# Gate, up and down products of a transformer block in one region with a fixed order of engines, shared accumulators and spread operand sums

## The chip, the cores and the metric

The kernel runs on one core of one Trainium2 chip. The metric is the device time of one execution in microseconds, the median of several. A profile is one execution; its span is a few microseconds off the median.

Engines are named as in the profile: PE is TensorE's matrix products, PEld its weight loads, DVE VectorE, ACT ScalarE, SP SyncE, which issues the transfers. A name such as L753 is a line of the kernel.

## The reference, cut to what matters

One transformer block over 2048 tokens of 1024 features, in bfloat16: a linear-attention part, then a gated feed-forward part of 3584 features. The change touches only the second part.

```python
def _B_ref(x, W_gate, W_up, W_down):
    gate = jnp.einsum("bsd,df->bsf", x, W_gate)     # (2048,1024) @ (1024,3584)
    up = jnp.einsum("bsd,df->bsf", x, W_up)
    gate = gate * (gate > 0)
    h = gate * up
    return jnp.einsum("bsf,fd->bsd", h, W_down)     # (2048,3584) @ (3584,1024)

h2 = h + _B_ref(_layernorm(h), W_gate, W_up, W_down)
```

## The kernel before

All large products use Strassen's scheme in Winograd's form: of two 2x2 block matrices, 7 block products and sums of operands and results instead of 8 products. So TensorE is not the only busy engine: VectorE makes sums of operands ahead of the products and adds accumulators to saved copies ("snaps") behind them.

**Gate/up.** There are 24 windows. One window is 7 products ("1" to "7") of 8 matmuls of 128x512 each. Product 1 goes to accumulator A, is copied out (a snap), and 6, 7 and 4 are added into the same A, with a snap after 6 and after 7. Product 2 goes to D; 5 and later 3 go to E. Each accumulator holds 128x1024 float32 values in PSUM; I call its place a pair of banks, one half for gate and one for up. A alternates between two places; D and E have one place each. `prev` is the last part of the previous window, put between the first and second part of this one. `fill` holds sums that the down product will want; one is taken per window from the fifth on. A scheduler decides each engine's order from this text. The results are stored to DRAM ("spilled") and loaded again by down as its operand x.

```python
    apools = [ps2, ps2b]                                   # A alternates, D and E do not
    def part1():
        st["A"] = A = apools[k % len(apools)].tile([P, 2, SW], FP32, tag="A", name="A")
        prod(A, 1, True)
        m1 = snap(A)                                       # ScalarE copy
        Dp = ps2.tile([P, 2, SW], FP32, tag="D", name="Dp")
        prod(Dp, 2, True)
        finish_sum(Dp, m1, 0)                              # VectorE: gu = D + m1, then hq = relu(gate)*up
    def part2():
        A = st["A"]
        prod(A, 6, False)
        st["u2"] = snap(A)
        st["E"] = E = ps2.tile([P, 2, SW], FP32, tag="E", name="E")
        prod(E, 5, True)
        prod(A, 7, False)
        finish_sum(E, snap(A), 3)
    def part3():
        ...  # product 4 into A and its result, product 3 into E, finish_sum(E, st["u2"], 1)
    # ... (cut) ...
        for s, f, wt_, fi in items:
            p1, p2, p3 = quad_steps(s, f, w[fi] if w else sums(wt_, fi), k)
            k += 1
            p1()
            if prev:
                prev()
            p2()
            if k > 4 and fill:
                fill.pop(0)()
            prev = p3
```

**Down.** Seven outer products, in the order 1, 2, 6, 5, 7, 3, 4. Two of them (1 and 7) are plain: 4 accumulators of 28 matmuls of 128x512, half of them before and half after the second half of the operands. The other five are Strassen again: 7 products of 28 matmuls of 128x256. Their operand sums (t1 to t4 of weights, s1 to s4 of activations) are made on VectorE from tiles loaded just before, in this order, and taken from a list `pend` at fixed places:

```python
        return [
            lambda: tt(out=t1, in0=b12, in1=b11, op=ALU.subtract),
            lambda: tt(out=t2, in0=b22, in1=t1, op=ALU.subtract),
            lambda: tt(out=s1, in0=a21, in1=a22, op=ALU.add),
            ...  # s2, s3, t3, t4, s4
        ]
    # ... (cut) ...
        if k in INNER:
            p1, p2, p3 = inner(op, *plans[k])
            p1()
            if prev:
                prev()
            some(3)
            p2()
            some(8)
            prev = p3
```

An output piece (a "sink" in the code) is two VectorE sums (`o` = accumulator + snap, then + the residual) and a store issued on the SP queue.

Of the kernel before, what the change touches and what calls it, by code (L numbers as in the profile page):

```python
# [31 lines left out]
def block_kernel(ctx: ExitStack, tc: tile.TileContext, x, wqkv, wo, wg, wu, wd, out, H: int):  # L32
# [542 lines left out]
    def weight_sums(w_sb, fi, nm):  # L575

        b = [[w_sb[:, k * KH:(k + 1) * KH, h, fi * P:(fi + 1) * P] for h in range(2)] for k in range(2)]
        t = tpool.tile([P, 4, KH, P], FP16, tag=nm, name=nm)
        nc.vector.tensor_tensor(out=t[:, 0], in0=b[0][1], in1=b[0][0], op=ALU.subtract)
        nc.vector.tensor_tensor(out=t[:, 1], in0=b[1][1], in1=t[:, 0], op=ALU.subtract)  # L580
        nc.vector.tensor_tensor(out=t[:, 2], in0=b[1][1], in1=b[0][1], op=ALU.subtract)
        nc.vector.tensor_tensor(out=t[:, 3], in0=b[1][0], in1=t[:, 1], op=ALU.subtract)
        return b[0][0], b[1][0], b[1][1], t[:, 3], t[:, 0], t[:, 1], t[:, 2]
# [3 lines left out]
    def wd_sums(c):  # L587

        raw = spool[0].tile([P, 2, 2, D], BF16, tag="wraw", bufs=1, name="wraw")
        for k in range(2):  # L590
            nc.sync.dma_start(out=raw[:, k], in_=wd_k[:, k, 2 * c:2 * c + 2, :])
        t = spool[0].tile([P, 4, 2, DW], FP16, tag="wt", bufs=1, name="wt")
        (b11, b12), (b21, b22) = [[raw[:, k, :, j * DW:(j + 1) * DW] for j in range(2)] for k in range(2)]
        nc.vector.tensor_tensor(out=t[:, 0], in0=b12, in1=b11, op=ALU.subtract)
        nc.vector.tensor_tensor(out=t[:, 1], in0=b22, in1=t[:, 0], op=ALU.subtract)
        nc.vector.tensor_tensor(out=t[:, 2], in0=b22, in1=b12, op=ALU.subtract)
        nc.vector.tensor_tensor(out=t[:, 3], in0=b21, in1=t[:, 1], op=ALU.subtract)
        for k in range(4):
            nc.sync.dma_start(out=t_dram[k][:, 2 * c:2 * c + 2, :], in_=t[:, k])
# [21 lines left out]
    def early_sums(f):  # L621

        k, r = divmod(f, FQ)
        hq = new_hq()
        nc.sync.dma_start(out=x1[0][k][:, r, :], in_=raw_dram[0][:, f, :])
        for q, j in ((3, H22), (2, H21), (1, H12)):
            nc.sync.dma_start(out=hq[:, j, :], in_=raw_dram[q][:, f, :])
        hh_sums_a(hq, 0, f)
        hh_sums_b(hq, 0, f)

    def quad_steps(s, fc, w, k):

        left = left_ops(hnT[s], hns[s])

        def prod(ps, m, start):
            for v in range(2):
                for kc in range(KH):
                    nc.tensor.matmul(ps[:, v, :], lhsT=w[v][m - 1][:, kc, :], rhs=left[m - 1][:, kc, :],  # L638
                                     start=(start and kc == 0), stop=(kc == KH - 1), skip_group_check=True)

        slots = {1: H12, 2: H21, 3: H22}
        is_early = k is None
        hq = None if is_early else new_hq()

        def dst(q):
            if is_early:
                return mwork.tile([P, SW], BF16, tag="hh1", bufs=4, name="hh1")[:]
            if q in slots:
                return hq[:, slots[q], :]
            return x1[s][fc // FQ][:, fc % FQ, :]  # L650

        def spill(q, ap):
            if is_early:
                nc.sync.dma_start(out=raw_dram[q][:, fc, :], in_=ap)
            elif q == 2:
                hh_sums_a(hq, s, fc)
            elif q == 1:
                hh_sums_b(hq, s, fc)

        def snap(ps):  # L660
            m = mwork.tile([P, 2, SW], FP32, tag="snap", bufs=4, name="snap")
            nc.scalar.copy(out=m[:], in_=ps[:])  # L662
            return m

        def finish_sum(ps, m, q):
            gu = mwork.tile([P, 2, SW], BF16, tag="gu", name="gu")
            nc.vector.tensor_tensor(out=gu[:], in0=ps[:], in1=m[:], op=ALU.add)  # L667
            d = dst(q)
            nc.scalar.activation(out=gu[:, 0, :], in_=gu[:, 0, :], func=ACT.Relu)  # L669
            nc.vector.tensor_tensor(out=d, in0=gu[:, 0, :], in1=gu[:, 1, :], op=ALU.mult)  # L670
            spill(q, d)

        st = {}

        def narrow():

            gus = {}

            def mm(ps, m, v, start):
                for kc in range(KH):  # L680
                    nc.tensor.matmul(ps[:], lhsT=w[v][m - 1][:, kc, :], rhs=left[m - 1][:, kc, :],
                                     start=(start and kc == 0), stop=(kc == KH - 1), skip_group_check=True)

            def fin(i, j, v, ps, m):
                q = 2 * i + j
                if v == 0:
                    gus[q] = mwork.tile([P, 2, SW], BF16, tag="gu", name="gu")
                gu = gus[q]
                if m is not None:
                    nc.vector.tensor_tensor(out=gu[:, v, :], in0=ps[:], in1=m, op=ALU.add)  # L690
                if v == 0:
                    nc.scalar.activation(out=gu[:, 0, :], in_=ps[:] if m is None else gu[:, 0, :], func=ACT.Relu)
                else:
                    d = dst(q)
                    nc.vector.tensor_tensor(out=d, in0=gu[:, 0, :], in1=ps[:] if m is None else gu[:, 1, :], op=ALU.mult)
                    spill(q, d)

            return strassen(pspool, mwork, mm, fin, 4)

        def part1():  # L700
            st["A"] = A = apools[k % len(apools)].tile([P, 2, SW], FP32, tag="A", name="A")
            prod(A, 1, True)
            m1 = snap(A)
            Dp = ps2.tile([P, 2, SW], FP32, tag="D", name="Dp")
            prod(Dp, 2, True)
            finish_sum(Dp, m1, 0)

        def part2():
            A = st["A"]
            prod(A, 6, False)  # L710
            st["u2"] = snap(A)
            st["E"] = E = ps2.tile([P, 2, SW], FP32, tag="E", name="E")
            prod(E, 5, True)
            prod(A, 7, False)
            finish_sum(E, snap(A), 3)

        def part3():
            A, E = st["A"], st["E"]
            prod(A, 4, False)
            rg = mwork.tile([P, SW], BF16, tag="rg", name="rg")  # L720
            nc.scalar.activation(out=rg[:], in_=A[:, 0, :], func=ACT.Relu)
            d = dst(2)
            nc.vector.tensor_tensor(out=d, in0=A[:, 1, :], in1=rg[:], op=ALU.mult)  # L723
            spill(2, d)
            prod(E, 3, False)
            finish_sum(E, st["u2"], 1)

        return narrow if k is None else (part1, part2, part3)

    def sums(wt, fi):  # L730
        return [weight_sums(wt[0], fi, "tg"), weight_sums(wt[1], fi, "tu")]
# [3 lines left out]
    for f in range(NE):  # L735
        st = {}

        def begin(f=f, st=st):
            st["q"] = quad_steps(0, f, sums(early[f // GP], f % GP), None)()
            next(st["q"])  # L740

        flow += [begin] + [lambda st=st: next(st["q"])] * 5
# [13 lines left out]
    ps2ctx = ExitStack()  # L756
    ps2 = ps2ctx.enter_context(tc.tile_pool(name="ps2", bufs=1, space=PSUM))
    apools = [ps2, ps2ctx.enter_context(tc.tile_pool(name="ps2b", bufs=1, space=PSUM))]
    x1pool = ctx.enter_context(tc.tile_pool(name="x1pool", bufs=4, side="right"))
    prepool = ctx.enter_context(tc.tile_pool(name="prepool", bufs=1, side="right"))  # L760
    sctx = ExitStack()
    spool.append(sctx.enter_context(tc.tile_pool(name="spool", bufs=1, side="right")))
# [4 lines left out]
    x1 += new_x(x1pool)  # L767

    todo = [[(1, f, early[f // GP], f % GP)] for f in range(NE)]
    todo += [[(s, g * GP + fi, g, fi) for s in range(NS) for fi in range(GP)] for g in range(NE // GP, FH // GP)]  # L770
    fill = [lambda f=f: early_sums(f) for f in range(NE)] + [lambda c=c: wd_sums(c) for c in range(FH // 2)]
    prev, k = None, 1
    for n, items in enumerate(todo):
        w = {}
        if n >= NE:
            wt, loads = load_group(items[0][2])
            for f in loads:
                f()
            w = {fi: sums(wt, fi) for fi in range(GP)}
# [3 lines left out]
        for s, f, wt_, fi in items:  # L783
            p1, p2, p3 = quad_steps(s, f, w[fi] if w else sums(wt_, fi), k)
            k += 1
            p1()
            if prev:
                prev()
            p2()
            if k > 4 and fill:  # L790
                fill.pop(0)()
            prev = p3
# [291 lines left out]
```

## Time and profile before

| | before |
|---|---|
| median time, three executions | 771.17 us (767.87 to 772.5) |
| span of the profiled run | 767.4 us |
| first matmul of gate/up starts at | 298.2 us |
| last matmul of gate/up | 601.7 us |
| last matmul | 761.4 us |
| holes of TensorE in gate/up | 13.3 us |
| holes of TensorE in down | 4.4 us |

The page gives TensorE's busy share:

```profile
PE 728.2 (95%) x4004; PEld 380.7 (50%) x4004; DVE 557.8 (73%) x1019; ACT 327.0 (43%) x597; POOL 6.1 (1%) x44
```

At 95% there seems to be little left. But the matmuls overlap in the record, so busy time is not work. I read starts instead: in the timeline a 128x512 matmul follows the last one after 0.216 us, a 128x256 one after 0.109 us, and what is above that is a hole. That is how all holes of this document are computed. (A group of matmuls in the timeline shows the idle time after the last one ended, which is 0.16 to 0.17 us less than the hole.)

The waits of TensorE, by what ended them; the columns are total us, number, longest us (only waits from 0.2 us or so are listed, so the sums are smaller than the holes):

```profile
engine line waited for: us in total, times, longest us
...
PE E L638 <- DVE gu L667: 5.0, 9, 1.5
...
PE accA L919 <- DVE snap L925: 2.8, 4, 1.3
...
PE A L638 <- DVE hq L723: 2.0, 5, 0.8
...
PE A L638 <- ACT snap L662: 1.1, 1, 1.1
```

L638 are the gate/up products: they wait for VectorE to free E (its sum `gu`) or A (`hq`). Two such holes in the timeline (start, length, engine, line, operation, count, and in brackets the idle time before with what ended it):

```profile
start us, us, engine line op out<-in xcount [idle before <-releaser]
...
380.37 1.02 PE L638 MATMUL A<-hn,wg 128*128 128x512 bf16 x4 [0.78 <-DVE hq L723]
...
383.85 1.02 PE L638 MATMUL E<-hs,tg 128*128 128x512 f16 x4 [1.16 <-DVE gu L667]
```

E's new product 5 waits for the sum that reads the old product 3 out of the same banks, because only one other product lies between them. And VectorE isn't always prompt. This is the view of stretches of 50 us (busy us of each engine with its number of instructions, the granted clock, the share of the transfer engines, GB/s):

```profile
core 0: us, PE busy (x) PEld busy (x) DVE busy (x) ACT busy (x) POOL busy (x), PEclk, DMA share, GB/s
...
350.00:400.00 50.00, 47.61 (x218) 21.13 (x217) 42.47 (x86) 20.42 (x27) 0.00 (x0) 1.00 0.94 307
...
450.00:500.00 50.00, 49.25 (x227) 21.95 (x226) 32.86 (x61) 21.25 (x29) 0.00 (x0) 1.00 0.35 106
...
600.00:650.00 50.00, 48.97 (x329) 32.02 (x328) 30.74 (x29) 5.59 (x7) 0.00 (x0) 1.00 0.86 320
```

VectorE is busy for 42.5 of 50 us at 350 to 400 us, where the down sums are bunched, and for 32.9 us at 450 to 500 us. TensorE runs 218 and 227 matmuls in these stretches, where 231 would fit.

### The profile page before, as it was taken

The page shows a single profiled execution, that of the slowest core. Times are in us where ns is not written, and L with a number is a line of the kernel's source. Part 1 is how long each engine was busy: PE and PEld are TensorE (multiplying, and loading weights), DVE is VectorE, ACT ScalarE, POOL GpSimd, SP SyncE. Part 2 cuts the span into 40 slices and gives each one's busy share as a digit, 9 for nine tenths or more (in the row PEclk, how much of TensorE's full clock was granted, in tenths as well). Part 3 has the DMA queues.
Part 4 walks back from the last instruction along what each step waited for, and adds up shares of the span by engine and source line. Part 5 has one row for each costly group of instructions (what it writes and reads, how often), then busy time and mean ns, then how long its engine had stood idle before and what let it go on. Part 6 is the DMA issues. An engine that isn't in the chain of part 4 may idle for free.

```text
span 767.4 us, 10597 instructions
## 1 busy us (share of the span) xinstructions
PE 728.2 (95%) x4004; PEld 380.7 (50%) x4004; DVE 557.8 (73%) x1019; ACT 327.0 (43%) x597; POOL 6.1 (1%) x44
## 2 busy tenths in 40 slices
PE   5999999999889999999999999999999999999996
PEld 2444555444344444444344444444444468885785
DVE  5997654786896767799797575675756359967994
ACT  4776553878777554444344434344444120000000
POOL 0000000000000000000000000000000000000000
PEclk9999999999999999999999999999999999999999
DMA  9675003079767536589896143252121598997823
GB/s 318 148 138 151 1 1 108 4 171 224 188 157 194 121 112 203 197 282 310 297 303 187 55 126 108 82 151 83 41 83 63 172 401 316 348 344 236 306 63 89
DMA packets 146403, 132.03 MB, mean 172 GB/s; under 512 B 50864, under 2 KB 127920, under 8 KB 146352
## 3 DMA queue, kind: packets, MB, share of 16 engines
q1 hardware_dynamic: 146352, 131.36, 56.3%
q8 instruction: 31, 0.51, 0.3%
q14 instruction: 20, 0.16, 0.1%
HBM read 79.95 MB, written 39.85 MB: 156 GB/s over the span
## 4 chain that ended last, share of the span: by engine, by line
PE 26%; DVE 21%; DMA 5%; ACT 4%; issue 3%; SPq 2%; DVEq 0%; ACTq 0%
PE A L638 7%; DVE gu L667 6%; PE accA L919 6%; PE E L638 4%; PE accE L919 3%; DVE hq L723 2%; DMA x<-x_dram 2%; DMA hq<-raw_dram 2%; ACT gu L669 2%; ACT snap L662 2%; PE accA L963 2%; PE Dp L638 1%; DMA wraw<-in_B_W_down_dram 1%; PE accD L919 1%; DVE hq L606 1%
## 5 line engine op out<-in xcount | busy, mean ns | idle before, releaser
L662 ACT COPY snap<-A 128x1024 f32<-128x1024 f32 x72 | 72.3, 1013 | 124.5 <-PE A L638 124.1
L667 DVE TENSOR_TENSOR gu<-E,snap 128x1024 bf16<-128x1024 f32 x48 | 58.6, 1220 | 48.0 <-ACT snap L662 48.0
L669 ACT ACTIVATE gu<-gu 128x512 bf16<-128x512 bf16 x72 | 45.4, 631 | 53.3 <-DVE gu L667 53.1
L638 PEld LDWEIGHTS <-tg 128*128 128x128 f16 x384 | 37.4, 97 | 56.0 <-issue 13.6
L517 PE MATMUL attn<-wo_mem,oT 128*128 128x512 bf16 x256 | 57.8, 379 | 3.4 <-DVE o_sb L497 3.1
L638 PEld LDWEIGHTS <-tu 128*128 128x128 f16 x384 | 37.5, 98 | 45.3
L919 PEld LDWEIGHTS <-x 128*128 128x128 f16 (+1 forms) x560 | 54.8, 98 | 9.1 <-issue 2.2
L152 ACT COPY u<-Aq 128x512 f32<-128x512 f32 x56 | 32.2, 581 | 44.8 <-PE Aq L285 21.2
L638 PE MATMUL A<-hn,tg 128*128 128x512 f16 (+1 forms) x192 | 49.4, 379 | 1.1 <-ACT snap L662 1.1
L638 PE MATMUL A<-hn,tu 128*128 128x512 f16 (+1 forms) x192 | 49.6, 379 | 0.0
L638 PEld LDWEIGHTS <-wg 128*128 128x128 bf16 x288 | 28.1, 98 | 37.2 <-issue 3.4
L638 PEld LDWEIGHTS <-wu 128*128 128x128 bf16 x288 | 28.2, 98 | 34.0
L919 PEld LDWEIGHTS <-xs 128*128 128x128 f16 x420 | 41.1, 98 | 7.0 <-issue 2.2
L517 PEld LDWEIGHTS <-oT 128*128 128x128 bf16 x256 | 24.9, 97 | 35.0 <-issue 6.7
L670 DVE TENSOR_TENSOR hq<-gu 128x512 bf16<-128x512 bf16 x48 | 20.2, 421 | 22.5 <-ACT gu L669 22.5
L963 PEld LDWEIGHTS <-x 128*128 128x128 bf16 (+1 forms) x224 | 21.9, 98 | 26.0
L919 PE MATMUL accA<-w,x 128*128 128x256 f16 (+1 forms) x280 | 32.2, 273 | 0.3 <-DVE snap L925 0.2
L285 PEld LDWEIGHTS <-xT 128*128 128x128 bf16 (+1 forms) x192 | 18.6, 98 | 25.2 <-issue 3.7
L667 DVE TENSOR_TENSOR gu<-Dp,snap 128x1024 bf16<-128x1024 f32 x24 | 29.3, 1220 | 1.3 <-PE Dp L638 1.3
L638 PE MATMUL E<-hs,tg 128*128 128x512 f16 x96 | 24.6, 377 | 5.7 <-DVE gu L667 5.0
L497 DVE TENSOR_TENSOR o_sb<-nd,rd 128x384 bf16<-128x384 f32 (+1 forms) x48 | 22.8, 507 | 8.6 <-ACT rd L496 8.3
L638 PE MATMUL A<-hn,wg 128*128 128x512 bf16 x96 | 27.1, 379 | 2.0 <-DVE hq L723 2.0
(189 smaller groups left out, 1361.7 us busy)
## 6 DMA issues: line engine op xcount, KB each, us to landing
x<-x_dram SPq DMA_DIRECT2D x24, 896.0 KB, 8.4
x_dram<-hq SPq DMA_DIRECT2D x28, 512.0 KB, 2.9
wg<-in_B_W_gate_dram SPq DMA_DIRECT2D x14, 512.0 KB, 5.1
wu<-in_B_W_up_dram SPq DMA_DIRECT2D x14, 512.0 KB, 6.1
wraw<-in_B_W_down_dram SPq DMA_DIRECT2D x14, 512.0 KB, 4.7
t_dram<-wt SPq DMA_DIRECT2D x28, 256.0 KB, 2.4
x_dram<-hq SPq DMA_DIRECT2D x28, 256.0 KB, 2.5
w<-t_dram SPq DMA_DIRECT2D x8, 896.0 KB, 5.8
```

What stands on the lines that cost most here:

```text
L152: nc.scalar.copy(out=snaps[nm, v], in_=A[v][:])
L285: nc.tensor.matmul(ps[:], lhsT=left[m - 1][:, kc, r + v * P:r + (v + 1) * P], rhs=right[m - 1][:, kc, :], start=(start and kc == 0), stop= ...
L497: nc.vector.tensor_tensor(out=ov[:, c0:c0 + n], in0=ndv[:, :, 0:P].rearrange("p k (h e) -> p k h e", h=HPC), in1=rd[:, 0:n, :].unsqueeze(3 ...
L517: nc.tensor.matmul(ps[:], lhsT=st["oT"][:, c, :], rhs=wo_sb[:, c, j * NW:(j + 1) * NW], start=(c == 0), stop=(c == KC - 1))
L638: nc.tensor.matmul(ps[:, v, :], lhsT=w[v][m - 1][:, kc, :], rhs=left[m - 1][:, kc, :], start=(start and kc == 0), stop=(kc == KH - 1), ski ...
L662: nc.scalar.copy(out=m[:], in_=ps[:])
L667: nc.vector.tensor_tensor(out=gu[:], in0=ps[:], in1=m[:], op=ALU.add)
L669: nc.scalar.activation(out=gu[:, 0, :], in_=gu[:, 0, :], func=ACT.Relu)
L670: nc.vector.tensor_tensor(out=d, in0=gu[:, 0, :], in1=gu[:, 1, :], op=ALU.mult)
L723: nc.vector.tensor_tensor(out=d, in0=A[:, 1, :], in1=rg[:], op=ALU.mult)
L919: nc.tensor.matmul(pv[:, tt, :], lhsT=op["left"][m - 1][:, f, tt * P:(tt + 1) * P], rhs=op["right"][m - 1][:, f, :], start=(start and f == ...
L963: nc.tensor.matmul(pss[p][:, t * NW:(t + 1) * NW], lhsT=op["x"][s][kh][:, f, (t0 + t) * P:(t0 + t + 1) * P], rhs=op["w"][kh][:, f, :], sta ...
```

## The change

The intent: no hole in gate/up, by three means. D and E share one pair of banks, X or Y, that alternates by window, so three products (one for E before) lie between the last product into a pair and the next one that starts in it. The order of TensorE, VectorE and ScalarE is the order of the text, which interleaves this window's products, the last parts of the previous window, and small pieces ("slots") of the operand sums. The down sums are cut into pieces and spread over the windows. In down the same pool and the same kind of order are used; the loads are placed by hand; output stores go to ScalarE's queue; the first half of the first accumulator of down is put before the tail of the last gate/up window; the last Strassen product gets its own banks for its tail.

The diff, cut to its core (`...` marks cuts):

```diff
-    apools = [ps2, ps2ctx.enter_context(tc.tile_pool(name="ps2b", bufs=1, space=PSUM))]
+    accs = ctx.enter_context(tc.tile_pool(name="accs", space=PSUM, **reuse))
+    ctx.enter_context(tc.manual_schedule(engines={ET.PE, ET.DVE, ET.Activation}))
+    def acc(tag):
+        return accs.tile([P, 2 * NW], FP32, tag=tag, bufs=2 if tag == "A" else 1, name="acc" + tag)
...
+    def quad(s, fc, w, k):
+        tag = "XY"[k % 2]
...
+            "m1": lambda: m(1, "A", "A"), "s1": lambda: snap("m1"), "m2": lambda: m(2, "D", tag),
+            "g0": lambda: gu(0, "D", "m1"), "x0": lambda: mul(0), "m6": lambda: m(6, "A"), "s2": lambda: snap("u2"),
+            "m5": lambda: m(5, "E", tag), "m7": lambda: m(7, "A"), "s3": lambda: snap("u3"),
...
+    fill = [p for f in range(NE) for p in early_sums(f)] + [p for c in range(FH // 2) for p in wd_sums(c)]
...
+            cur["m1"]()
+            cur["s1"]()
+            if prv:
+                prv["g3"](); slot(0); prv["x3"]()      # (joined to one line here)
+            cur["m2"]()
+            if prv:
+                prv["m4"]()
+            cur["g0"]()
...                                                     # x0, rg, m6, slot(2), x2, s2, prv m3, slot(3), m5, prv g1, m7, s3
+    plain_mm(first_ps[0], xfirst, wfirst, 0, 0)         # first 14 matmuls of down
+    prv["g3"]()                                         # tail of the last gate/up window
...
+        queue.extend((op, f.__name__, f) for f in (t1, s1, s2, t2, s3, t3, t4, s4))
...
-        nc.sync.dma_start(out=out_v[...], in_=ov)
+        nc.scalar.dma_start(out=out_v[...], in_=ov)
...
+            cur["m1"]()                                 # one Strassen product of down
+            if prv:
+                prv["11"]()
+                pop()                                   # pop: one operand sum of the next product
+            cur["s1"]()
...
+            cur["m6"]()
+            if prv:
+                prv["01"]()
+            pop()
+            ...
+            cur["m5"]()
+            cur["s2"]()
+            pop(2)
+            cur["m7"]()
+            pop(2)
+            if tail:
+                ...                                     # own banks: "m4f", "10f"; last sink in halves "01a", "01b"
```

## The prediction

> **What bounds it now.** TensorE: 95% busy on the page, but its matmuls overlap, so I read starts in the timeline: a 128x512 matmul follows the last after 0.216 us, a 128x256 one after 0.109 us (the Trainium skill, "TensorE: Matmul & The Clock Gate", Part 2, gives one column per cycle, 213 ns; the trace is 1% above). Start to start, all matmuls need 714 us; 40 us are holes. Half lie before 299 us, where the order stays. Within reach, summed from the timeline:
> - gate/up, 299 to 602 us: 13.3 us, nearly all released by "DVE gu", "DVE hq" or a snap copy: there is one E and one D buffer, and VectorE is 85% busy at 350 to 400 us, where the down-weight sums are bunched, 61 to 68% later.
> - down, 602 to 762 us: 4.4 us, 1.4 of them at 635 and 640 us behind "DVE snap", 1.5 at 755 us.
> - after the last matmul: 5.7 us (VectorE 1.22 and 0.69, then a 2.3 us store).
>
> **What the change does.** Arithmetic stays, but for one more snap and halved last sinks. D/E buffers alternate, each engine's order is fixed, fill sums spread over 20 windows, output stores move to ScalarE's queue. ("PSUM — Partial Sum Buffer", section "Engine vs sequencer instructions": ScalarE and VectorE queues are strict FIFO; no view shows that directly.)
>
> **Gate/up.** A window is 56 matmuls, 12.1 us. VectorE needs 3 x 1.22 + 3 x 0.42 + 0.69 + 4 x 0.42 (sums for spill) + 4 x 0.42 (weight sums) = 9.0 us, plus 1 to 2 of fill: it fits. Every accumulator is free 2 us or more before TensorE wants it. Holes fall from 13.3 to about 1 us: -12.3.
>
> **Entry of down.** Here I expect a loss. 3.0 us of its first product now run before the last window's tail and no longer cover the loads. On the SP queue an extra 896 KB x load, which waits for TensorE, precedes the second half of the first weights. In the trace these loads land every 2.2 to 2.6 us after a first 5. From the end of gate/up that puts the weights at 10.8 us, wanted at 9.1 (hole 1.7); the first Strassen product's snap, behind eight sums that wait for x, ends at 33 us, wanted at 29 (hole 4); the next snap waits for an x load (hole 1). Later, two ops need 23 to 25 us of VectorE in 21 to 24 us: 1 to 3 us more. Down holes: 4.4 to about 9.5: +5.1.
>
> **End.** The last product's own banks remove the 1.5 us hole, the extra snap gives 0.8 back (both counted above); halved last sinks: -0.9.
>
> **Sum.** 767.4 - 12.3 + 5.1 - 0.9 = 759.3 us of span; by ratio to the median, 763 us. 8 in 10: 754 to 769. Faster by over 2%: 0.17; within: 0.80; slower: 0.03.
>
> **What would show it.** Gate/up: "gu" and "hq" gone as releasers of TensorE, 231 matmuls per 50 us instead of 219 to 227. Down: TensorE waiting for "w" and "DVE snap" in its first 45 us; VectorE waiting for x loads. End: under 5 us after the last matmul.
>
> **What would make it wrong.** VectorE's fixed order stalls in gate/up on a down-weight load (single buffers) beyond 2 to 3 us of slack: slower. Or the x loads land sooner: then all 18 us of holes go and it nears 752.

## The result, and the profile after

| | before | after |
|---|---|---|
| median time, same rounds | 770.33 us | 762.45 us (761.17 to 764.18) |
| ratio | | 0.99, 95% interval 0.9862 to 0.9938 |
| span of the profiled run | 767.4 us | 761.0 us |

The prediction was 763.0 us, within 2%: the time was right. The spans say it more strictly: 759.3 us predicted, 761.0 us measured, so a gain of 6.3 us instead of 8.1. A ratio here is the mean time of one kernel's runs over that of the other's runs of the same rounds, so it is not quite the ratio of the medians that are quoted. Executions over 1.5% slower than the fastest of the same kernel are left out of the means.

The spans, cut into stretches by the starts of matmuls in the timeline:

| stretch | before | after | difference |
|---|---|---|---|
| start to first gate/up matmul | 298.2 | 297.1 | -1.1 |
| gate/up, without the 3.0 us of down that now run inside it | 303.5 | 289.9 | -13.6 |
| down, with those 3.0 us | 159.7 | 168.3 | +8.6 |
| from the last matmul's start to the end | 6.0 | 5.7 | -0.2 |
| sum | 767.4 | 761.0 | -6.3 |

The first row is noise. The text of that part is unchanged, and in the runs below gate/up starts anywhere from 297.0 to 300.5 us.

TensorE's waits after (columns as before):

```profile
engine line waited for: us in total, times, longest us
...
PE accA L1042 <- DVE snap L1048: 5.3, 4, 3.8
...
PE accA L885 <- DMA w<-in_B_W_down_dram: 3.0, 1, 3.0
...
PE accY L1042 <- DMA out_dram<-o: 1.1, 1, 1.1
...
...
```

VectorE's `gu` and `hq` are gone as releasers in gate/up. All listed here is in down. The stretches of 50 us (columns as before), and at the end one of 3.4 us:

```profile
350.00:400.00 50.00, 49.79 (x229) 22.69 (x232) 37.54 (x72) 21.56 (x29) 0.00 (x0) 1.00 0.52 154
...
450.00:500.00 50.00, 49.74 (x229) 22.62 (x232) 39.73 (x73) 21.77 (x30) 0.00 (x0) 1.00 0.66 204
...
600.00:650.00 50.00, 43.36 (x327) 32.59 (x328) 36.93 (x29) 4.05 (x4) 0.00 (x0) 0.97 1.00 368
```

```profile
624.50:627.90 3.40, 2.78 (x14) 1.92 (x14) 3.27 (x4) 0.00 (x0) 0.00 (x0) 0.50 1.02 418
```

VectorE is even: 37.5 and 39.7 of 50 us. The counts of 229 matmuls are short because of missing records (53 are missing in the whole trace; the weight loads, 232 per stretch, are all there). 24 windows of 56 matmuls need 24 x 56 x 0.216 = 290.3 us, and gate/up took 289.9: there is no hole left in it. At 600 to 650 us the picture turns: VectorE busier, the transfer engines at a share of 1.00, TensorE 5.6 us less busy than before.

The entry of down on TensorE (timeline columns as before):

```profile
596.26 3.19 PE L885 MATMUL accY<-b,x 128*128 128x512 bf16 x14
602.48 6.20 PE L885 MATMUL accA<-w,x 128*128 128x512 bf16 x28 [3.03 <-DMA w<-in_B_W_down_dram]
...
615.00 3.23 PE L1042 MATMUL accA<-w,x 128*128 128x256 bf16 x28 [0.27 <-DMA x<-x_dram]
618.07 3.22 PE L1042 MATMUL accY<-w,x 128*128 128x256 bf16 x28
625.12 4.56 PE L1042 MATMUL accA<-ws,xs 128*128 128x256 f16 x28 [3.83 <-DVE snap L1048]
629.52 3.22 PE L1042 MATMUL accY<-ws,xs 128*128 128x256 f16 x28
```

And on VectorE:

```profile
605.10 1.09 DVE L960 TENSOR_TENSOR ws<-w 128x1792 f16<-128x1792 bf16 x1 [11.05 <-DMA w<-in_B_W_down_dram]
612.15 2.02 DVE L973 TENSOR_TENSOR xs<-x 128x3584 f16<-128x3584 bf16 x1 [5.96 <-DMA x<-x_dram]
615.03 2.03 DVE L976 TENSOR_TENSOR xs<-xs,x 128x3584 f16<-128x3584 f16 x1 [0.86 <-DMA x<-x_dram]
...
621.92 2.02 DVE L983 TENSOR_TENSOR xs<-x,xs 128x3584 f16<-128x3584 bf16 x1
623.85 1.22 DVE L1048 TENSOR_TENSOR snap<-accA,u 128x1024 f32<-128x1024 f32 x1
```

There are two large holes. At 602.48 us (3.2 us) TensorE waits for the second half of the first weights. At 625.12 us (4.0 us) it waits for a snap that VectorE made at 623.85 us. The product that the snap reads had been done since about 618.2 us. The snap stands behind eight sums in VectorE's queue: VectorE makes the first at 605.10 us, then waits for x loads ahead of the second (5.96 us) and the third (0.86 us), and makes the rest one after the other.

The product after that hole took 4.56 us where its neighbour of the same 28 matmuls took 3.22 us. The row of 624.5 to 627.9 us shows the granted clock: 0.50. In the trace the clock is halved for 3.41 us, and 13 matmuls started 0.213 us apart instead of 0.109 us: 1.4 us lost. The Trainium skill, "TensorE: Matmul & The Clock Gate", Part 1, section "What's actually happening", states this: a clock of half the rate after an idle window of about 3.4 us, with free-running windows of 3413 ns. Trace and page agree on the half and on 3.41 us; on the idle time see the last section. The trace of before has no such record between 290 and 765 us.

The tail on VectorE, after the last matmuls (the two halves of the last sink, each a sum with the snap and one with the residual):

```profile
755.62 0.69 DVE L1007 TENSOR_TENSOR o<-accX,snap 128x512 bf16<-128x512 f32 x1 [0.72 <-PE accX L1042]
...
757.41 0.42 DVE L1008 TENSOR_TENSOR o<-o,h 128x512 bf16<-128x512 bf16 x1
```

### The profile page after: what moved, and what is told of

It is laid out like the page before. It is cut to its first block, busy times and chain, and to the rows that moved or that the text cites. A ratio compares the mean times of both kernels' runs of the same rounds, so it can differ in the third digit from the quotient of the medians.

```text
span 761.0 us, 10554 instructions
## 1 busy us (share of the span) xinstructions
PE 721.2 (95%) x3951; PEld 381.3 (50%) x4004; DVE 565.7 (74%) x1022; ACT 326.5 (43%) x597; POOL 6.1 (1%) x44
## 4 chain that ended last, share of the span: by engine, by line
PE 65%; DVE 16%; DMA 9%; ACT 5%; issue 2%; SPq 1%; POOL 0%; DVEq 0%; ACTq 0%
PE accA L753 22%; PE accX L753 8%; PE accY L753 8%; DMA x<-x_dram 5%; PE accA L1042 4%; PE attn L517 4%; PE Aq L285 3%; PE Aq L419 2%; PE Eq L285 2%; PE Aq L673 2%; PE accX L1042 2%; PE accY L1042 2%; DVE stats L254 2%; DVE o L1007 1%; DMA hn<-hn 1%
## 5 line engine op out<-in xcount | busy, mean ns | idle before, releaser
L758 ACT COPY snap<-accA 128x1024 f32<-128x1024 f32 x72 | 72.7, 1010 | 44.9 <-PE accA L753 44.8
L762 DVE TENSOR_TENSOR gu<-accY,snap 128x1024 bf16<-128x1024 f32 x36 | 43.9, 1220 | 10.2 <-ACT snap L758 10.2
L753 PE MATMUL accA<-hn,tg 128*128 128x512 f16 (+1 forms) x192 | 49.3, 379 | 0.0
L753 PE MATMUL accA<-hn,tu 128*128 128x512 f16 (+1 forms) x192 | 49.3, 379 | 0.0
L762 DVE TENSOR_TENSOR gu<-accX,snap 128x1024 bf16<-128x1024 f32 x36 | 43.9, 1220 | 7.0 <-ACT snap L758 3.9
L1048 DVE TENSOR_TENSOR snap<-accA,u 128x1024 f32<-128x1024 f32 x16 | 19.4, 1219 | 11.5 <-PE accA L1042 11.5
L519 DVE SCALAR_TENSOR_TENSOR x_res<-attn,x_res 128x512 bf16<-128x512 f32 x32 | 22.0, 688 | 6.3 <-PE attn L517 6.2
```

Of the source, the lines that this page charges most:

```text
L519: nc.vector.scalar_tensor_tensor(out=h_sb[:, j * NW:(j + 1) * NW], in0=ps[:], scalar=1.0, in1=h_sb[:, j * NW:(j + 1) * NW], op0=ALU.mult, ...
L753: nc.tensor.matmul(ps[:, v, :], lhsT=w[v][n - 1][:, kc, :], rhs=left[n - 1][:, kc, :], start=(t is not None and kc == 0), stop=(kc == KH - ...
L758: nc.scalar.copy(out=st[nm][:], in_=halves(st["A"]))
L762: add(out=g[:], in0=halves(st[nm]), in1=st[base][:], op=ALU.add)
```

## The experiments

Each is one edit to the changed kernel, but e7 adds to e1, e6 and e8 add to e7, and e9 joins e5 and e2. All gave the right result. The spans differ in the start, as said, so the fourth column is from the first gate/up matmul to the end in the profiled run. "Halved clock" counts only records of the gate/up and down stretches (290 to 750 us; in e4 to 810 us). A hole of about 1.25 us at 713 to 719 us (e4: 783 us), behind the bank pair of the next product, is in every run but before and e8 and is left out of the column.

| run | median us | ratio to before, 95% | first gate/up matmul to end | large holes of TensorE: us at time | halved clock, us |
|---|---|---|---|---|---|
| before | 770.33 | 1 | 469.1 | many of 0.3 to 1.7 in gate/up | 0 |
| after | 762.45 | 0.990 (0.9862 to 0.9938) | 463.9 | 3.2 at 602, 4.0 at 625 | 3.41 |
| e1_tfirst | 767.52 | 0.9973 (0.9944 to 1.0002) | 466.0 | 2.8 at 604, 1.0 at 624, 4.0 at 634, 2.2 at 659 | 3.41 |
| e2_p0after | 765.38 | 0.9939 (0.9907 to 0.9971) | 465.9 | 1.3 at 586, 1.3 at 621, 4.1 at 631, 3.2 at 656 | 3.41 |
| e3_sporder | 767.56 | 0.9972 (0.9944 to 1.0001) | 468.5 | 0.4 at 600, 1.0 at 613, 4.0 at 623, 3.5 at 727 | 10.24 |
| e4_noalt | 831.07 | 1.0793 (1.0753 to 1.0833) | 531.8 | one in almost every window | 37.5 (10 places) |
| e5_nomanual | 759.64 | 0.9867 (0.9848 to 0.9886) | 460.4 | 2.8 at 605, 1.0 at 625, 1.1 at 663 | 0 |
| e7_snapfirst | 761.01 | 0.988 (0.9861 to 0.9899) | 460.3 | 2.9 at 604, 1.0 at 624, 1.0 at 654 | 0 |
| e6_snapfirst_p0 | 758.37 | 0.9858 (0.9835 to 0.988) | 459.5 | 1.3 at 588, 2.8 at 640 | 3.41 |
| e8_best | 757.99 | 0.9836 (0.9818 to 0.9854) | 459.3 | 1.3 at 586, 2.5 at 638, 1.7 at 742 | 3.41 |
| e9_sched_p0 | 758.07 | 0.9868 (0.9847 to 0.989) | 459.7 | 1.7 at 604, 1.0 at 624, 1.2 at 663 | 0 |
| e10_spstore | 765.49 | 0.9937 (0.9914 to 0.9961) | 467.7 | 3.2 at 604, 4.0 at 627, 1.7 at 659 | 6.83 |
| e11_wholesink | 764.08 (1 run) | | 464.9 | 2.9 at 602, 3.5 at 626 | 6.83 |

### What made the gain in gate/up

**e4_noalt: D always in X, E always in Y, as before.**

```diff
-  "m2": lambda: m(2, "D", tag),
+  "m2": lambda: m(2, "D", "X"),
-  "m5": lambda: m(5, "E", tag),
+  "m5": lambda: m(5, "E", "Y"),
```

> One edit to the changed kernel: in gate/up product D always uses bank pair X and E always Y, as before the change; order and all else stay. If the second E buffer is what makes the hand order work, product 5 must wait in each of 23 windows for the add that reads E after product 3 of the window before: 0.2 + 1.22 us, so about 1.4 us a window, 33 us in all: span about 794. If the order alone takes the holes away and the buffers matter little: span under 765.

The time rose to 831.07 us, and gate/up alone from 292.9 to 359.8 us. TensorE's largest wait is now this:

```profile
PE accY L753 <- DVE gu L762: 48.1, 23, 3.4
```

In the new order the previous window's product 3 is followed at once by this window's product 5. With one E both want the same banks, and TensorE waits for the sum that lies between them: 23 waits of 2.1 us on average. So the order of the changed kernel needs the alternating pairs. The size was missed: about 33 us were expected and a span of 794 us. The holes in gate/up came to 52 us (2.3 us each, not 1.4), and the nine halved windows there, 30.7 us long, make up the other 15 of the 66.9 us; why the sum comes later than expected was not followed up. This run doesn't show that the pairs are enough without the fixed order; the next one does. One of these waits, and what came of it:

```profile
363.36 1.02 PE L753 MATMUL accY<-hs,tg 128*128 128x512 f16 x4 [2.18 <-DVE gu L762]
364.22 1.62 PE L753 MATMUL accY<-hs,tu 128*128 128x512 f16 x4
365.63 1.91 PE L753 MATMUL accA<-hn,tg 128*128 128x512 f16 x4
```

An idle time of 2.18 us was followed by a halved clock from 364.51 us on (the 8 matmuls from 364.22 us on took 3.3 us instead of 1.9). The same idle time of 2.18 us at 393.15 us had no such record. More on this in the last section.

**e5_nomanual: the fixed order of engines taken away.** The scheduler orders all engines again, from the new text with its pairs.

```diff
-    ctx.enter_context(tc.manual_schedule(engines={ET.PE, ET.DVE, ET.Activation}))
```

> One edit to the changed kernel: the hand order is not enforced; the compiler's scheduler orders TensorE, VectorE and ScalarE again, with the change's PSUM pool (D and E in alternating bank pairs). It keeps TensorE's products of gate/up in the change's order but bunches the down-weight sums on VectorE early, as before the change. If the second E buffer is what takes the holes of gate/up away: gate/up still takes about 290 us from its first to its last product, holes under 3 us. If the spread of the sums and the fixed order of VectorE are needed: half or more of the 13 us of holes of before come back. For down, where the scheduler may put snaps ahead of sums that wait for loads: the holes of 4 us before product 6 fall to about 1.

It was not slower: 759.64 us; the interval of its ratio overlaps that of the changed kernel, so "faster" is not shown. The scheduler gave TensorE the same order of products in gate/up, but VectorE the sums in bunches as before:

```profile
350.00:400.00 50.00, 49.41 (x226) 22.38 (x229) 41.83 (x81) 20.70 (x29) 0.00 (x0) 1.00 0.83 260
```

VectorE is at 41.8 of 50 us in the bunched stretch and TensorE runs 226 matmuls there (229 weight loads, so some records are missing), against 218 before. The holes of all of gate/up came to about 1 us (0.3 at 301 and 304 us, 0.5 at 395 us). So neither the fixed order nor the spreading of sums was needed for the gain. What is common to this run and the changed kernel is the pairs and the text's order of products; the pairs with the old order of products were not run, so which of the two is needed beside the other is shown only in one direction (e4). In down the scheduler's order also took the hole of 4.0 us before the first snap to 1.0 us.

### Where the gain went: the entry of down

The theory after the result: both large holes are of order. The first is of the order of loads, with 3 us of cover taken away; the second is of VectorE's queue, where the snap stands behind sums that wait for loads. The rival: the loads are simply too slow for this stretch (the transfer share is 1.00), and any order only moves the hole.

**e1_tfirst: the sums of the first Strassen product in another order, those that need only weights first.**

```diff
-  queue.extend(... for f in (t1, s1, s2, t2, s3, t3, t4, s4))
+  order = (t1, t2, t3, t4, s1, s2, s3, s4) if op["n"] == 1 else (t1, s1, s2, t2, s3, t3, t4, s4)
+  queue.extend(... for f in order)
```

> One edit to the changed kernel: of the eight operand sums of the first Strassen product of down, the four weight sums go first on VectorE, the four token sums after. Nothing else moves. Theory A (the loss at the entry of down comes from the fixed order of VectorE's queue, which makes the first snap stand behind sums that need not be late): VectorE does the weight sums in the 11 us in which it waits for x in the changed kernel, the first snap ends near 622 instead of 625 us, TensorE's hole before product 6 falls from 4.0 us to about 1, the halved clock after it (3.4 us, worth 1.4 us) is gone: span about 756.7, 4.3 less than 761.0. Rival B (the entry is bound by the loads: the DMA share is 1.00 from 600 to 650 us, so a later wait for a load gives back what is won): span within 1 us of 761.

The time was 767.52 us: slower than the changed kernel. The timeline of TensorE shows why:

```profile
623.55 3.22 PE L1043 MATMUL accA<-ws,xs 128*128 128x256 f16 x28 [0.83 <-DVE snap L1049]
626.60 3.22 PE L1043 MATMUL accY<-ws,xs 128*128 128x256 f16 x28
633.63 6.57 PE L1043 MATMUL accA<-w,x 128*128 128x256 f16 x45 [3.81 <-DVE snap L1049]
```

The hole in front of the first Strassen product's snap fell from 4.0 to 1.0 us, because VectorE now makes three sums of weights while it waits for x. But the hole came back in full two products later: 4.0 us at 633.63 us, again behind a snap, with a halved clock. VectorE at this place:

```profile
630.42 2.03 DVE L973 TENSOR_TENSOR xs<-x 128x3584 f16<-128x3584 f16 x1 [3.87 <-DMA x<-x_dram]
632.36 1.22 DVE L1049 TENSOR_TENSOR snap<-accA,u 128x1024 f32<-128x1024 f32 x1
```

It waits 3.87 us for an x load of the next product, makes a sum from it, and only then the second snap, at 632.36 us. Product 6, which that snap reads, had ended at about 626.8 us. Here the rival is right in part: to mend one place moves the hole. It doesn't say yet whether the loads or the queue are at fault.

**e7_snapfirst: e1, and the second snap too ahead of the next product's sums.** The sums that were taken between the sink "01" and product 5 are taken after the second snap.

```diff
             cur["m6"]()
             if prv:
                 prv["01"]()
-            pop()
             ...
             cur["m5"]()
             cur["s2"]()
-            pop(2)
+            pop(3)
```

> The kernel of e1 (weight sums first) with one more edit: in every Strassen product of down, the second snap stands on VectorE ahead of the next product's token sums, not behind the first of them. e1 moved the hole from product 6 (4.0 to 1.0 us) to product 7 (0 to 4.0 us, and 2.2 us one product later), where a snap of a product long done stood behind a token sum that waited 4 us for its load. Theory A2 (queue order: each snap must stand ahead of sums that wait for loads): those holes and the clock dips go, from e1's span about 4.0 + 2.2 + 1.4 = 7.6 less: about 757; the hole for the weights (2.8 to 3.2 us) stays. Rival B (bound by loads): the hole moves on again, span 763 to 765.

TensorE, and then VectorE, at the same place:

```profile
624.23 3.22 PE L1043 MATMUL accA<-ws,xs 128*128 128x256 f16 x28 [0.83 <-DVE snap L1049]
627.28 3.22 PE L1043 MATMUL accY<-ws,xs 128*128 128x256 f16 x28
630.34 6.28 PE L1043 MATMUL accA<-w,x 128*128 128x256 f16 x56
```

```profile
627.48 1.23 DVE L1049 TENSOR_TENSOR snap<-accA,u 128x1024 f32<-128x1024 f32 x1 [0.27 <-PE accA L1043]
631.18 2.03 DVE L973 TENSOR_TENSOR xs<-x 128x3584 f16<-128x3584 f16 x1 [2.48 <-DMA x<-x_dram]
```

VectorE makes the second snap at 627.48 us and waits for the x load after it. TensorE goes from 624.23 to 640 us without a break, no clock record is halved, and the time is 761.01 us, against 767.52 us for e1. The x load did not come sooner: VectorE could begin its sum at 631.18 us, against 630.42 us in e1. So this hole of 4 us was made by VectorE's queue, not by the speed of the loads. A snap that is ready must not stand behind a sum that waits for a transfer. The Trainium skill, "PSUM — Partial Sum Buffer", section "Engine vs sequencer instructions", calls VectorE's queue a strict FIFO; the traces agree, since VectorE stood idle for 3.87 us in e1 with a snap ready behind the sum.

Down, without the part of it that runs inside gate/up, took 161.7 us here against 165.3 us in the changed kernel: 2.3 us are holes, 1.4 us the clock. Against the changed kernel's times the gain is not clear (the intervals overlap); the hole behind the weights and five of about 1 us stay.

**e2_p0after: the first 14 matmuls of down put back behind the tail of the last gate/up window.**

```diff
-    plain_mm(first_ps[0], xfirst, wfirst, 0, 0)
     prv["g3"]()
     ...
     prv["x1"]()
+    plain_mm(first_ps[0], xfirst, wfirst, 0, 0)
```

> One edit to the changed kernel: the 3.0 us of the first down product that ran before the tail of the last gate/up window run after it, as before the change. Theory A (the piece put in front delays the last spill of gate/up by 3 us and with it all loads and sums that down waits for, and lets an x load slip ahead of the first weights): the loads are issued 3 us sooner and the weights first, the hole for the weights (3.2 us) goes, the one before product 6 falls from 4.0 to about 2 with no clock dip; the tail pays about 1.3 us for its snap: span about 755, 6 less than 761. Rival C (the piece in front pays, for it hides the tail's waits for copies): span 762.3 or more, 1.3 us over.

The hole behind the weights is gone. But two things changed with this edit: the 14 matmuls cover the loads again, and no x load stands ahead of the weights on the SP queue any more. The weights landed 5.1 us after their issue (593.97 to 599.11 us), against 8.0 us in the changed kernel (594.48 to 602.44 us). e3 below keeps the move and changes the order alone. A hole of 1.3 us came in the tail at 586 us, which the move had hidden. The hole behind the first snap fell from 4.0 to 1.3 us, but one of 4.1 us came behind the second snap at 631 us, as in e1 (VectorE waits 4.01 us for an x load first), and one of 3.2 us at 656 us. In sum it was 765.38 us, not better than the changed kernel. With the queue as it is, TensorE only arrives earlier at the next wait.

**e6_snapfirst_p0: e7 and e2 together.**

```diff
(the edits of e7_snapfirst and of e2_p0after)
```

> As e7, and the 3.0 us of the first down product run after the last window's tail, as in e2. Theory A2: e2's holes for snaps of 1.2, 4.1 and 3.2 us and its clock dip of 1.4 us go, and no hole for the weights is left: from e2's span of 764.2 about 9.9 less, 754.5. Rival B: the hole moves on, span 761 or more.

Together they do what e2 alone didn't: 758.37 us, ratio 0.9858. From e7 it can't be told apart (the intervals overlap), and the expected span of 754.5 us was not reached (754.9 to 760.0 us). The profiled run was the slowest of its five (761.76 us), with a late start of gate/up at 300.5 us. A hole of 2.8 us at 640 us behind the next product's snap remains.

**e3_sporder: the SP queue in the order of the text too.**

```diff
-    engines={ET.PE, ET.DVE, ET.Activation}
+    engines={ET.PE, ET.DVE, ET.Activation, ET.SP}
```

> One edit to the changed kernel: SyncE's queue of loads and spills is held to the program's order too, so that no x load stands ahead of the first down weights. Theory A: the weights and all x loads of the entry land about 2.2 us sooner, the hole for the weights falls from 3.2 to about 1 us, the hole before product 6 stays 3 to 4 us; span about 758, if the order does no harm elsewhere in gate/up. Rival B (bound by the loads' total, whose order does not matter): span within 1 us of 761.

In the changed kernel the scheduler had put an x load of the next product (issued at 593.4 us) ahead of the second half of the first weights (issued at 594.5 us, landed at 602.4 us). With the order of the text the hole behind the weights was 0.4 us instead of 3.2. So the move without a load ahead leaves only 0.4 of the 3.2 us. A load ahead without the move would leave little too, by an estimate from the changed kernel: the weights landed 12.4 us after the end of gate/up and were wanted at 9.1 us, which 3.0 us of cover would make 12.1 us. The hole takes both. The entry gained 2 us in this way: product 6, behind the first snap, began at 622.87 instead of 625.12 us, though still behind a hole of 4.0 us. What was lost came after it: 3.5 us at 727 us, where a snap again stands behind a sum that waits (3.44 us) for an x load, and a clock halved for 10.24 us in sum: 767.56 us.

**e8_best: e6, and in the plain product 7 the next product's sums only after its first two accumulators.** The aim is the wait of 1.25 us for the bank pair at 713 us and the snaps behind it.

```diff
-                pop(2)
+                pop(2 if p < 2 else 0)
```

> As e6, and in the plain product of down (the fifth) VectorE does two of the next product's sums after each of the first two sinks only, none after the last two, so that its last bank pair comes free sooner. In all runs so far the next product stood 1.25 us for that bank pair and 0.97 us for a snap behind the sums, and 0.6 later. Theory A2: these fall to about 0.5 in sum, so about 2 us less than e6: span 752.5. Rival: the sums put off come due in the next product, and span stays within 0.5 us of e6.

It was 757.99 us, ratio 0.9836, the lowest; its interval lies below those of e7, the changed kernel and before, and overlaps those of e5, e6 and e9. Its entry of down and its remaining large hole:

```profile
599.69 2.32 PE L885 MATMUL accY<-b,x 128*128 128x512 bf16 x10
601.85 6.21 PE L885 MATMUL accA<-w,x 128*128 128x512 bf16 x28
...
637.85 4.83 PE L1043 MATMUL accA<-ws,x 128*128 128x256 f16 x28 [2.35 <-DVE snap L1049]
```

TensorE now passes from gate/up into down without a hole until 637.85 us, where a snap comes late by 2.5 us; the product behind it took 4.83 us because of a halved clock. VectorE shows the same pattern as in e1, at a snap that e7 had not moved:

```profile
628.64 2.02 DVE L973 TENSOR_TENSOR xs<-x 128x3584 f16<-128x3584 f16 x1 [4.11 <-DMA x<-x_dram]
...
636.58 1.22 DVE L1049 TENSOR_TENSOR snap<-accA,u 128x1024 f32<-128x1024 f32 x1
```

This is the third snap, of product 7, which had ended at about 629.4 us. Five sums stand ahead of it, and the first of them waited 4.11 us for its load. No run moved this snap. Of the third edit little was kept: at 710 us only 0.3 us are left of the 2.2 us that it was aimed at, but 1.7 us came at 742 us, where VectorE had been busy without a pause since 713 us. From the first gate/up matmul to the end it is 0.2 us less than e6, so the rival of this expectation (the sums that are put off come due later) held.

**e9_sched_p0: the scheduler's order (e5) and the first matmuls put back (e2).**

```diff
(the edits of e5_nomanual and of e2_p0after)
```

> The changed kernel with the fixed engine order taken away (the scheduler orders all engines) and the first product's first 14 matmuls put back behind the last gate/up window. Theory (the gain comes from the alternating bank pairs, the loss at the entry of down from the order of loads and queues): gate/up stays at 290 to 294 us with holes of about 1 us, the 2.8-us hole behind the weights at 604 us of the run with the scheduler alone is gone as it went when this edit was made to the changed kernel, a hole of about 1.2 us behind the tail's copy stays; span from the first gate/up matmul to the end 458 to 460 us, median 756 to 759 us, against 759.6 for the scheduler alone. Rival (the scheduler would put the loads in the same order whatever the text says, so the hole in the weights stays): 460 to 461 us, median within 0.1% of 759.6.

The ratio, 0.9868, is that of e5 (0.9867). The hole behind the weights shrank from 2.8 to 1.7 us and did not go; the theory had expected it gone. The trace shows why: the scheduler ran 4 of the 14 matmuls ahead of the tail all the same, and an x load (596.8 us) was still issued ahead of the weights (597.1 us, landed at 604.3 us). Gate/up to the end took 459.7 us, in the range that the theory gave; the median of 758.07 us can't be told from e5's.

### Two smaller parts of the change

**e10_spstore: output stores on the SP queue again.**

```diff
-        nc.scalar.dma_start(out=out_v[...], in_=ov)
+        nc.sync.dma_start(out=out_v[...], in_=ov)
```

> The changed kernel with its output stores issued on the SP queue again. If moving the stores to the ScalarE queue matters (they no longer stand behind loads that wait), x loads of the middle of down come later by some tenths of a microsecond and holes of TensorE after 640 us grow by 1 to 3 us: median 764 to 766 us. If it does not matter, the holes after 640 us stay at 4 us in sum and the median stays within 0.2% of 762.5 us. The entry of down (600 to 635 us), which has no output store yet, is the same under both.

The holes after 640 us rose from 3.9 to 5.8 us (1.7 instead of 0.4 at the snap at 659 us, 1.1 instead of 0.7 at 730 us). The median of 765.49 us lies in the range for "it matters", but the intervals of the two ratios overlap, the profiled run was the slowest of the six (768.41 us), and 1.4 to 1.7 us of the span are a second halved window at 626 us, before any store. So the stores' move is worth perhaps 2 us; one trace shows it and the times leave it open. The Trainium skill, "DMA: Bandwidth & Descriptors", section "Issuing engines are not separate DMA queues", says that another issuing engine only saves the time that issuing takes. The other way in which a store could matter is by waiting for its data in the queue and holding up the loads behind it. The trace has one such case: the store issued at 643.75 us waited for VectorE until 643.73 us, and the x load behind it left at 644.23 us. The changed kernel issued that load at 638.88 us, 0.2 us after the start of a product that starts 3.8 us later here, so it left 1.6 us late. How much of the hole at 659 us this makes stays open: the load that VectorE then waited for (2.43 us) was issued in time at 648.78 us and took 7.5 instead of 5.0 us to land.

**e11_wholesink: the last sink in one piece.**

```diff
-                cur["01a"]()
-                cur["01b"]()
+                cur["01"]()
```

> The changed kernel with the last sink in one piece instead of two halves. The trace of the changed kernel has the two halves back to back on VectorE, 0.69 + 0.43 + 0.68 + 0.42 = 2.2 us, where one piece took 1.22 + 0.69 = 1.9 us before; so the time from the start of the last matmul to VectorE's last instruction should fall by 0.3 us here, and the last store, twice as large, take back about 0.5 us: 5.9 to 6.0 us from the last matmul's start to the end, against 5.7. If the halving was worth the 0.9 us that was predicted, it would be 6.6 us. One look; the time itself cannot tell.

```profile
756.64 1.22 DVE L1007 TENSOR_TENSOR o<-accX,snap 128x1024 bf16<-128x1024 f32 x1 [0.72 <-PE accX L1042]
757.90 0.69 DVE L1008 TENSOR_TENSOR o<-o,h 128x1024 bf16<-128x1024 bf16 x1
```

VectorE ends its part 1.95 us after it began, against 2.21 us for the halves in the changed kernel. From the last matmul's start to the end it took 5.98 us, against 5.71 us: the halves cost 0.3 us on VectorE and get back about 0.5 us by a smaller last store. So halving is worth 0.3 us: this stretch took 5.68 to 5.71 us in all eleven traces with the halves, and 5.96 us in the trace of before.

## Why the prediction was right

The time was right, 763.0 us against 762.45 us, and so was its shape: a gain in gate/up, part of which the entry of down gives back (5.1 of 12.3 us predicted, 8.6 of 13.6 us measured). But terms of the sum were off, and they cancelled in part: gate/up and the noise before it gave 2.4 us more than predicted, down and the end 4.2 us less. That the median came within 0.6 us is partly luck; the span was 1.7 us off.

| term | predicted us | measured us |
|---|---|---|
| before gate/up | 0 | -1.1 (noise) |
| gate/up | -12.3 | -13.6 |
| down: hole behind the weights | 1.7 | 3.2 |
| down: hole behind an x load before the first Strassen product | 0 | 0.4 |
| down: hole behind its first snap | 4 | 4.0 |
| down: next snap | 1 | 0.4 |
| down: later (bank pair 1.25, snaps 0.97 and 0.67) | 1 to 3 | 2.9 |
| down: extra snap of the tail | 0.8 | 0.7 |
| down: halved clock | 0 | 1.4 |
| down, holes and clock of before | -4.4 | -4.4 |
| down, sum | +5.1 | +8.6 |
| end | -0.9 | -0.2 |

- **"Holes fall from 13.3 to about 1 us: -12.3."** Right, and a little too careful: none is left. The reason given there (the pairs, the fixed order and the spread sums) was too wide. e5 shows that the holes go without the fixed order and with bunched sums; e4 shows that the order without the pairs is worse than before by 8%.
- **"Hole 1.7" behind the weights.** The mechanism was right: the moved 3.0 us and the x load ahead on the queue, which takes both (e3: with the load behind, 0.4 us; e2: with neither, no hole). The size was off. The weights were reckoned at 10.8 us after the end of gate/up and landed at 602.4 - 590.0 = 12.4 us.
- **"The first Strassen product's snap, behind eight sums that wait for x: hole 4."** Right in size and cause. With the weight sums made during the wait for x (e1), 3.0 of the 4.0 us go. But the queue does the same at the next snap, which e1 met and e7 mended; I had put only 1 us there.
- **The step that failed: the cost of a hole.** A hole was counted at its length. After a hole the clock can be halved for 3.41 us, which cost another 1.4 us here. Before had holes of at most 1.7 us from 290 us on and no halved record there, so its trace couldn't show that. The page on the clock gate (first point of the last section) could have warned: the predicted hole of 4 us is longer than the idle window of about 3.4 us that it names.
- **"Halved last sinks: -0.9."** Mis-sized. The two halves are in series on VectorE and longer in sum (2.2 against 1.9 us). Only the smaller last store gains. e11: 0.3 us.
- **"Under 5 us after the last matmul"** was wrong for the same reason: 5.4 us from its end, as the prediction reckoned, 5.7 us from its start. **"231 matmuls per 50 us"** can't be read off directly for the missing records; the weight loads show it (232).
- **The doubt that did not come true:** VectorE's fixed order did not stall gate/up on a down-weight load.

What stays open: whether the third snap, moved ahead too, would fill the hole at 638 to 640 us of e6 and e8; what the pairs give with the old order of products; and how much the stores' queue is worth.

## What to carry to other kernels

When an accumulator is read by one engine and refilled by another, ask first whether it has a second place: here the gain fell away without the alternating bank pairs, and with them even the scheduler's order left almost no hole. When a stage is sped up, look at what the next stage was waiting for under its cover: here loads and operand sums of the next stage had been hidden by the old stage's time. In an in-order queue, put the copies that release the critical engine ahead of all work that waits for a transfer, at every such place at once: mending one only moves the hole, and a hole of two microseconds or more can cost a halved clock on top.

## What the Trainium skill lacked or had wrong

- "TensorE: Matmul & The Clock Gate", Part 1, section "What's actually happening", gives the halved clock "after ≥1 idle window (~3.4µs)". Here shorter idle times were enough: 2.18 us in e4 at 363.36 us, 2.35 us in e8 at 637.85 us. And it is not a matter of length alone. Cut the time of a trace into windows of 3.413 us, counted from its halved records. The 2.18 us of e4 before 363.36 us lie whole in the window that ends at 364.51 us, and the clock is halved from there; the 2.18 us before 393.15 us are divided at 391.81 us into 0.84 and 1.34 us, and it is not. The 3.03 us of the changed kernel before 602.48 us are divided at 600.60 us into 1.15 and 1.88 us: not halved; at the same place of e11, 2.70 us lie in one window: halved from 602.71 us. In the gate/up and down stretches of all 13 traces every one of the 20 halvings begins at the end of a window with 2.14 us or more of idle time, and no window with 2.05 us or less is followed by the begin of one. That a part of a window is enough is lacking.
- The same section calls the windows free-running at 3413 ns. The runs agree: in e4 the halved windows begin at 333.79, 364.51, 422.53 and 480.56 us, and the steps of 30.72, 58.02 and 58.03 us are 9, 17 and 17 times 3.413 us.
- "DMA: Bandwidth & Descriptors", section "Issuing engines are not separate DMA queues", speaks of the issuing time only. With the stores back on the queue of the loads, the holes after 640 us were 5.8 instead of 3.9 us in one trace. That a store that waits for its data holds up a load behind it on the same queue (1.6 us in e10 at 644.23 us) would be worth a sentence there; what it costs in time this study doesn't settle.
